# Sorted attention with a feed-forward layer: batch 2's q turned by transposing DMAs, the first output block turned in two parts, the v pieces one place earlier

## The chip, the cores and the metric

The kernel runs on one core of a Trainium2 chip. Its time is the device time of one execution in microseconds. Before the change the median of 5 runs is 237.19 us (236.79 to 237.53). Engines are named as in the profile: PE does the matrix multiplications, PEld is its weight load, DVE, ACT and POOL work on vectors, and SP issues DMAs. POOL issues DMAs too; SP's and POOL's go through separate DMA queues.

## The reference

Four batches of eight heads, 768 rows (S) of 64 columns (D). A small `sort_net` becomes an 8 x 8 mixing matrix P per head through five rounds of exponentials and normalisations. P mixes the eight 96-row blocks of k and of v. Then each 96-row block of q attends to its own mixed block:

```python
k_sorted = np.einsum('bhij,bhjcd->bhicd', P, k_b)     # the same for v
scores = scale * np.matmul(q_b, k_sb.transpose(0, 1, 2, 4, 3))
attn = exp(scores - max) / sum
x = np.matmul(attn, v_sb)      # as 3072 rows x 512 columns
h = x @ w_in                   # 512 -> 2048
g = s * relu(h)**2 + b
out = g @ w_out                # 2048 -> 512, float32
```

## The kernel before

The 3072 rows are cut into eight groups `t` of 384 rows, two per batch. Each group passes through attention (`s_piece` for the scores and their exponentials, `p_piece` for the product with v and its normalisation), a turn of its output X into XT, the first feed-forward product (`ffn1`, L450) and the second (`ffn2`, L494). The order on every engine is the order in which the program is written; no scheduler changes it. A `Queue` (L511) puts attention pieces of later groups into the slots between feed-forward products: `ffn2` calls it after every four matmuls, `ffn1` after every eight.

**How q is turned.** The scores need q with its columns on the partitions (`QT`). Batches 1 and 2 do it on PE: `q_piece` (L261) makes 24 transposes for two head pairs, and DVE or ACT copies the result out of PSUM. Batch 3 does it by DMA: `load_q` (L78) then reads q in six parts of 128 rows with runs of one head's 64 columns, and `q_turn` (L274) issues six transposing DMAs on SP, each waiting for its own part. The other batches' `load_q` is one read with runs of six rows (384 columns).

**How X is turned.** For groups 0 and 1 on PE (`t_piece`, L412), afterwards by one transposing DMA on SP (`x_turn`, L435). For the first two blocks of group 0, `t_piece(0, "v", 0, 2)` at L590 makes eight transposes into one PSUM tile, and DVE copies all of it to XT; `ffn1(0)` starts on that. `warm_up` (L179) puts matmuls on zeros between these steps.

**v of batches 2 and 3.** Six `v_piece2` (the list `V2`) multiply by P, ACT copies the result, and SP writes it to a DRAM tile `dv`. `v_read` (L356) reads it back in the layout the attention needs, in two DMAs per batch. For batches 2 and 3 POOL issues them (L650, L651), after a one-element copy `gate2` (L649) that makes POOL wait for XT[3], the turned output of group 3. After the reads POOL issues `load_q(3)`.

**The stretch the change touches** is the queue of `ffn2(0)` and `ffn2(1)` (L632 to L639), 24 pieces for 24 slots: `q_piece(1, 2)`, batch 1's k pieces, then in slot 6 the loads of k for batches 2 and 3 and of q for batch 2 with `bias_piece`; scores `S2(2, ..)`, `V2`, products `P2(2, ..)`, the DMA turn `T(2)` in slot 18, `q_piece(2, 0)` in slot 21, `T(3)` in slot 23 and `q_piece(2, 2)` in slot 24. Then follow `ffn1(2)`, which needs XT[2], `ffn1(3)`, and `ffn2(2)`, whose first slots hold batch 2's scores `S2(4, 0)` and whose fourth holds `P2(4, 0)`, the first to need `v_read(2)`.

PSUM is used as a ring of three double-bank tiles (`psa`) and a ring of two single-bank tiles (`psb`); the results of `ffn2` lie in `psb` until `flush` (L472) has them scaled by DVE and written out. `flush` starts only when `bias_piece` has made the bias.

Of the kernel before, what the change touches and what calls it, by code (L numbers as in the profile page):

```python
# [10 lines left out]
BF = mybir.dt.bfloat16  # L11
# [7 lines left out]
def kernel(  # L19
# [12 lines left out]
    nc = tc.nc  # L32

    B, H, S, D = q.shape
    NB = sort_net.shape[-1]
    BLK = S // NB
    BH = B * H
    NHP = H // 2
# [4 lines left out]
    TG = HB * BLK  # L43
# [15 lines left out]
    xtp = ctx.enter_context(tc.tile_pool(name="xtp", bufs=2))  # L59
# [6 lines left out]
    psa = ctx.enter_context(tc.tile_pool(name="psa", bufs=3, space=bass.MemoryType.PSUM))  # L66
# [11 lines left out]
    def load_q(b, part=slice(0, 128)):  # L78


        if b == B - 1:
            qr[b] = qrp.tile([128, TQ, H, D], BF, tag="qr", name=f"qr{b}")
            for t in range(TQ):
                nc.gpsimd.dma_start(
                    out=qr[b][:, t],
                    in_=q[b][:, t * 128:(t + 1) * 128, :].rearrange("h p d -> p h d"))
            return
        if b not in qr:
            qr[b] = qrp.tile([128, H, TQ, D], BF, tag="qr", name=f"qr{b}")
        nc.gpsimd.dma_start(  # L90
            out=qr[b][part].rearrange("p h t d -> p h (t d)"),
            in_=q[b].rearrange("h (p t) d -> p h (t d)", t=TQ)[part])

    def load_k(rows, prow, n=1):
        for c0 in range(0, BLK, BLK // n):
            cs = slice(c0, c0 + BLK // n)
            nc.gpsimd.dma_start(out=kb[prow, cs, :], in_=kraw[rows, cs, :])
# [4 lines left out]
    def brows(b):  # L102
        return slice(b * 64, (b + 1) * 64), slice((b % 2) * 64, (b % 2) * 64 + 64)
# [26 lines left out]
    ident = const.tile([128, 128], BF)  # L130
# [21 lines left out]
    for c0 in range(0, d_ff, FCH):  # L152
        w = const.tile([128, NHP, FCH], BF, name=f"wi{c0}")
        nc.gpsimd.dma_start(
            out=w, in_=moe_w_in.rearrange("(hp p) f -> p hp f", p=128)[:, :, c0:c0 + FCH])
# [5 lines left out]
    for f0 in range(0, NF, FW):  # L161
        w = const.tile([128, FW, d_model], BF, name=f"wo{f0}")
        nc.gpsimd.dma_start(
            out=w, in_=moe_w_out.rearrange("(f p) n -> p f n", p=128)[:, f0:f0 + FW, :])
# [14 lines left out]
    def warm_up(n, pool=psb):  # L179
        wp = pool.tile([128, 256], FP, tag="b" if pool is psb else "a", name="wp")  # L180
        for _ in range(n):
            nc.tensor.matmul(out=wp, lhsT=zt[:, 0:128], rhs=zt, start=True, stop=True)  # L182
# [53 lines left out]
    def evac(out, in_, eng):  # L236
        if eng == "v":
            nc.vector.tensor_copy(out=out, in_=in_)  # L238
        else:
            nc.scalar.copy(out=out, in_=in_)  # L240

    QT = {}
# [18 lines left out]
    def q_piece(b, hp0, eng):  # L261

        if hp0 == 0:
            QT[b] = qtp.tile([128, NHP, S], BF, tag="qt", name=f"qt{b}")
        ps = psa.tile([128, 2, 1024], BF, tag="a", name="tq")
        for i in range(2):
            for t in range(TQ):
                for e in range(2):
                    nc.tensor.transpose(  # L269
                        out=ps[e * 64:(e + 1) * 64, i, t * 128:(t + 1) * 128],  # L270
                        in_=qr[b][:, 2 * (hp0 + i) + e, t, :], identity=ident)
        evac(QT[b][:, hp0:hp0 + 2, :].rearrange("q a (p t) -> q a p t", t=TQ),
             ps[:, :, 0:S].rearrange("q a (t p) -> q a p t", t=TQ), eng)

    def q_turn(b):

        QT[b] = qtp.tile([128, NHP, S], BF, tag="qt", name=f"qt{b}")
        for t in range(TQ):
            nc.sync.dma_start(out=QT[b][:, :, t * 128:(t + 1) * 128],
                              in_=qr[b][:, t].rearrange("p h d -> p (h d)"), transpose=True)  # L280
# [75 lines left out]
    def v_read(b, eng):  # L356
        if b > 1:
            new_vs(b)
        src = dv[1] if b == 1 else dv[2][(b - 2) * 64:(b - 1) * 64]
        for cp in range(2):  # L360
            eng.dma_start(out=VS[b][cp * (BLK // 2):(cp + 1) * (BLK // 2), :, 0:D],
                          in_=src.rearrange("g (c two) d -> two c g d", two=2)[cp])

    XT, AT, X = {}, {}, {}
# [16 lines left out]
    def p_piece(t, hp, n0=0, nn=HB):  # L381

        b, half = divmod(t, 2)
        at = AT[t, hp]
        if t not in X:
            X[t] = xp.tile([BLK, HB, d_model], BF, tag="x", name="x")
        x = X[t]
        atf = at.rearrange("p e t -> p (e t)")
        if nn < HB:
            p1 = psb.tile([128, 512], FP, tag="b", name="pv")  # L390
            pv = [p1[:, e * nn * VW:(e + 1) * nn * VW] for e in range(2)]
            pvv = p1[0:BLK, 0:2 * nn * VW].rearrange("p (e n w) -> p e n w", e=2, w=VW)
        else:
            p2 = psa.tile([128, 2, 512], FP, tag="a", name="pv")
            pv = [p2[:, 0], p2[:, 1]]
            pvv = p2[0:BLK, :, 0:nn * VW].rearrange("p e (n w) -> p e n w", w=VW)
        for e in range(2):
            for n in range(n0, n0 + nn):
                c0 = (e * HB + n) * BLK
                m = 128 if c0 + 128 <= 2 * TG else BLK  # L400
                gi = e * 32 + hp * NB + half * HB + n
                nc.tensor.matmul(out=pv[e][0:m, (n - n0) * VW:(n - n0 + 1) * VW],  # L402
                                 lhsT=atf[:, c0:c0 + m],
                                 rhs=VS[b][:, gi, :], start=True, stop=True)
        rec = rtp.tile([BLK, 2, HB], FP, tag="rec", name="rec")
        nc.vector.reciprocal(out=rec[:, :, 0:nn], in_=pvv[:, :, :, D])  # L406
        nc.vector.tensor_tensor(  # L407
            out=x[:, n0:n0 + nn, hp * 128:(hp + 1) * 128].rearrange("p n (e d) -> p e n d", e=2),
            in0=pvv[:, :, :, 0:D],
            in1=rec[:, :, 0:nn].unsqueeze(3).broadcast_to([BLK, 2, nn, D]), op=ALU.mult)  # L410

    def t_piece(t, eng, n0=0, nn=HB):  # L412

        x = X[t]
        if t not in XT:
            XT[t] = xtp.tile([128, NHP, TG], BF, tag="xt", name="xt")
        if nn < HB:
            t1 = psb.tile([128, 1024], BF, tag="b", name="tr")
            tr = [t1[:, hp * nn * BLK:(hp + 1) * nn * BLK] for hp in range(NHP)]
            src = t1[:, 0:NHP * nn * BLK]  # L420
            dst = XT[t][:, :, n0 * BLK:(n0 + nn) * BLK]
            src = src.rearrange("p (a t) -> p a t", a=NHP)
        else:
            t2 = psa.tile([128, 2, 1024], BF, tag="a", name="tr")
            tr = [t2[:, hp // 2, (hp % 2) * TG:(hp % 2 + 1) * TG] for hp in range(NHP)]
            src = t2[:, :, 0:2 * TG]
            dst = XT[t].rearrange("p (a b) t -> p a (b t)", b=2)
        for hp in range(NHP):
            for n in range(n0, n0 + nn):
                nc.tensor.transpose(out=tr[hp][:, (n - n0) * BLK:(n - n0 + 1) * BLK],  # L430
                                    in_=x[:, n, hp * 128:(hp + 1) * 128],
                                    identity=ident[0:BLK, 0:BLK])
        evac(dst, src, eng)

    def x_turn(t):  # L435

        XT[t] = xtp.tile([128, HB * NHP, BLK], BF, tag="xt", name="xt")
        nc.sync.dma_start(out=XT[t], in_=X[t].rearrange("p n m -> p (n m)"), transpose=True)
# [87 lines left out]
    def seq(*fs):  # L526
        def run():
            for f in fs:
                f()
        return run  # L530

    def S2(t, hp):
        return lambda: (s_piece(t, hp), s_piece(t, hp + 1))

    def P2(t, hp):
        return lambda: (p_piece(t, hp), p_piece(t, hp + 1))

    def T(t):
        return lambda: x_turn(t)
# [46 lines left out]
    s_piece(0, 3)  # L586
    for hp in range(NHP):
        p_piece(0, hp, 0, 2)
        warm_up(2, psa)
    t_piece(0, "v", 0, 2)  # L590
    warm_up(2, psa)

    load_v(*brows(2))
# [24 lines left out]
    def csums(f0, f1):  # L618
        for f in range(f0, f1):
            if f == 1:  # L620
                nc.gpsimd.tensor_tensor(out=csum, in0=wo_at(0), in1=wo_at(1), op=ALU.add)
            elif f > 1:
# [8 lines left out]
    V2 = [lambda c0=c0: v_piece2(c0, "s") for c0 in range(0, BLK, 16)]  # L631
    qu = Queue([nothing, lambda: q_piece(1, 2, "v")]  # L632
               + [lambda c0=c0: k_piece(1, c0, 16, 1, "vsv"[c0 // 32])() for c0 in range(0, BLK, 32)]
               + [seq(lambda: load_k(*brows(2)), lambda: load_k(*brows(3)), lambda: load_q(2), bias_piece), S2(2, 0), V2[0], S2(2, 2), V2[1], V2[2], V2[3],
                  P2(2, 0), V2[4], P2(2, 2), V2[5], S2(3, 0),
                  T(2), P2(3, 0), S2(3, 2), lambda: q_piece(2, 0, "v"), P2(3, 2), T(3),
                  lambda: q_piece(2, 2, "v")], 24)
    ffn2(0, qu)
    ffn2(1, qu)  # L639

# [5 lines left out]
    ffn1(2, qu)  # L646
    ffn1(3, qu)
    gate2 = sk.tile([1, 1], BF)
    nc.gpsimd.tensor_copy(out=gate2, in_=XT[3][0:1, 0, 0:1])  # L649
    v_read(2, nc.gpsimd)  # L650
    v_read(3, nc.gpsimd)  # L651
    load_q(3)
# [45 lines left out]
```

## Time and profile before

| | |
|---|---|
| median of 5 runs | 237.19 us |
| the profiled execution's own time | 236.81 us |
| its span | 235.1 us |
| PE busy | 227.7 us (97%) |
| DVE, ACT, POOL busy | 125.3, 111.3, 43.9 us |
| PE, L459 (ffn1) / L502 (ffn2) | 87.9 / 86.7 us |
| PE, L269 (`q_piece`), 96 transposes | 3.4 us |
| mean granted PE clock | 0.978 |

The span is what the profiler saw from the first to the last instruction; 1.7 us of the execution's time lie around it. Times below are microseconds from the span's start. The chain of waits is followed back from the last instruction, at each step to what released it. In a line of the timeline or chain the first number is the start and the second the length; "x8" is a count; a bracket says how long the engine had been idle and what ended that. A DMA has an issue (the time on SP or POOL) and a landing, counted from the start of the issue.

### The profile page before, as it was taken

The page shows a single profiled execution, that of the slowest core. Times are in us where ns is not written, and L with a number is a line of the kernel's source. Part 1 is how long each engine was busy: PE and PEld are TensorE (multiplying, and loading weights), DVE is VectorE, ACT ScalarE, POOL GpSimd, SP SyncE. Part 2 cuts the span into 40 slices and gives each one's busy share as a digit, 9 for nine tenths or more (in the row PEclk, how much of TensorE's full clock was granted, in tenths as well). Part 3 has the DMA queues.
Part 4 walks back from the last instruction along what each step waited for, and adds up shares of the span by engine and source line. Part 5 has one row for each costly group of instructions (what it writes and reads, how often), then busy time and mean ns, then how long its engine had stood idle before and what let it go on. Part 6 is the DMA issues. An engine that isn't in the chain of part 4 may idle for free.

```text
span 235.1 us, 4941 instructions
## 1 busy us (share of the span) xinstructions
PE 227.7 (97%) x2090; PEld 138.0 (59%) x2090; DVE 125.3 (53%) x259; ACT 111.3 (47%) x163; POOL 43.9 (19%) x57
## 2 busy tenths in 40 slices
PE   8979899999999999999999999999999999999994
PEld 5869797765544555555555455655554556554443
DVE  5758665638992658766344654343362544442221
ACT  6158369675148451677766221656322226660000
POOL 7810000299950000494000000000000000000000
PEclk9995699999999999999999999999999999999999
DMA  5799999998699996599992415420024162001112
GB/s 91 112 206 213 225 197 205 230 221 187 93 131 215 270 317 125 121 107 97 122 77 90 112 45 136 90 66 4 0 93 111 53 105 46 0 0 47 59 75 89
DMA packets 38230, 28.11 MB, mean 120 GB/s; under 512 B 26432, under 2 KB 32576, under 8 KB 37696
## 3 DMA queue, kind: packets, MB, share of 16 engines
q0 software_dynamic: 13600, 15.21, 45.2%
q1 hardware_dynamic: 24464, 12.53, 23.1%
q8 instruction: 16, 0.26, 0.5%
q10 hardware_dynamic: 144, 0.07, 0.1%
q14 instruction: 6, 0.05, 0.1%
HBM read 29.63 MB, written 8.65 MB: 163 GB/s over the span
## 4 chain that ended last, share of the span: by engine, by line
PE 83%; DVE 7%; DMA 5%; ACT 2%; issue 1%; POOL 0%; POOLq 0%
PE hps L459 35%; PE ops L502 32%; DMA qr<-in_q_dram 5%; PE pv L402 4%; PE sc L375 3%; DVE gt L464 2%; DVE ks L238 2%; PE tv L320 2%; PE tk L294 2%; PE ops L487 1%; ACT ks L240 1%; PE tv L350 1%; PE tq L269 1%; PE tq L254 1%; PE tv L336 1%
## 5 line engine op out<-in xcount | busy, mean ns | idle before, releaser
L459 PE MATMUL hps<-xt,wi 128*128 128x384 bf16 (+1 forms) x576 | 87.9, 308 | 0.7 <-DVE xt L238 0.4
L502 PE MATMUL ops<-wo,gt 128*128 128x512 bf16 x368 | 86.7, 380 | 0.0
L463 ACT ACTIVATE rt<-hps 128x768 bf16<-128x768 f32 (+1 forms) x72 | 53.2, 740 | 49.0 <-PE hps L459 48.1
L459 PEld LDWEIGHTS <-wi 128*128 128x128 bf16 x576 | 53.4, 98 | 30.6 <-issue 1.9
L464 DVE TENSOR_TENSOR gt<-rt 128x768 bf16<-128x768 bf16 (+1 forms) x72 | 41.2, 574 | 46.2 <-ACT rt L463 45.8
L502 PEld LDWEIGHTS <-gt 128*128 128x128 bf16 x368 | 33.7, 98 | 36.9 <-issue 0.6
L378 ACT ACTIVATE at<-sc 96x768 bf16<-96x768 f32 x32 | 24.4, 803 | 30.5 <-PE sc L375 30.3
L476 DVE SCALAR_TENSOR_TENSOR ot<-ops,s_bc,bias 128x512 f32<-128x512 f32 x23 | 17.2, 749 | 40.4 <-PE ops L502 40.3
L407 DVE TENSOR_TENSOR x<-pv,rec 96x512 bf16<-96x512 f32 (+1 forms) x36 | 22.6, 628 | 1.3
L240 ACT CAST ks<-tk 64x512 bf16<-64x512 f32 (+1 forms) x32 | 16.0, 500 | 6.4 <-PE tk L294 6.1
L238 DVE CAST ks<-tk 64x512 bf16<-64x512 f32 (+1 forms) x32 | 18.1, 565 | 1.3 <-PE tk L294 0.8
L623 POOL TENSOR_TENSOR csum<-csum,wo 128x512 f32<-128x512 f32 x14 | 17.6, 1255 | 1.0
L182 PE MATMUL wp<-zt 128*128 128x256 bf16 x92 | 14.7, 327 | 1.1 <-DVE warm L113 1.1
L402 PEld LDWEIGHTS <-at 96*128 96x128 bf16 (+1 forms) x256 | 12.0, 104 | 3.8
L402 PE MATMUL pv<-vs,at 96*128 96x66 bf16 (+1 forms) x256 | 13.0, 199 | 0.1
L375 PEld LDWEIGHTS <-ks 64*96 64x96 bf16 x256 | 8.5, 128 | 6.5 <-issue 5.7
L182 PEld LDWEIGHTS <-zt 128*128 128x128 bf16 x92 | 10.2, 116 | 3.4 <-DVE warm L113 1.1
L240 ACT CAST vn<-tv 128x512 bf16<-128x512 f32 (+1 forms) x12 | 9.4, 800 | 4.6 <-PE tv L350 3.9
L375 PE MATMUL sc<-qt,ks 64*96 64x96 bf16 x256 | 10.9, 219 | 0.6 <-DVE ks L238 0.5
L406 DVE RECIPROCAL rec<-pv 96x8 f32<-96x8 f32 (+1 forms) x36 | 6.9, 192 | 7.4 <-PE pv L402 7.4
L294 PEld LDWEIGHTS <-kb 64*128 64x128 bf16 x192 | 6.3, 95 | 4.5 <-issue 4.0
L294 PE MATMUL tk<-pd,kb 64*128 64x64 bf16 x192 | 7.8, 191 | 0.0
(70 smaller groups left out, 102.2 us busy)
## 6 DMA issues: line engine op xcount, KB each, us to landing
out_dram<-ot SPq DMA_DIRECT2D x23, 256.0 KB, 2.1
kb<-in_k_dram POOLq DMA_DIRECT2D x4, 768.0 KB, 11.1
vb<-in_v_dram POOLq DMA_DIRECT2D x4, 768.0 KB, 19.7
wi<-in_moe_w_in_dram POOLq DMA_DIRECT2D x2, 1024.0 KB, 20.4
wo<-in_moe_w_out_dram POOLq DMA_DIRECT2D x2, 1024.0 KB, 32.1
qr<-in_q_dram POOLq DMA_DIRECT2D x2, 768.0 KB, 26.6
dv<-vn SPq DMA_DIRECT2D x6, 256.0 KB, 8.0
vs<-dv POOLq DMA_DIRECT2D x4, 384.0 KB, 12.3
```

What stands on the lines that cost most here:

```text
L182: nc.tensor.matmul(out=wp, lhsT=zt[:, 0:128], rhs=zt, start=True, stop=True)
L238: nc.vector.tensor_copy(out=out, in_=in_)
L240: nc.scalar.copy(out=out, in_=in_)
L294: nc.tensor.matmul(out=ps[:, c, :], lhsT=kb[pr, c0 + 2 * c:c0 + 2 * c + 2, :].rearrange("p c d -> p (c d)"), rhs=rhs, start=True, stop=True)
L375: nc.tensor.matmul(out=sc[:, e, n * BLK:(n + 1) * BLK], lhsT=ks[pr, g0 + n, :], rhs=QT[b][pr, hp, q0:q0 + BLK], start=True, stop=True)
L378: nc.scalar.activation(out=at, in_=sc[:, :, 0:TG], func=AF.Exp, scale=scale)
L402: nc.tensor.matmul(out=pv[e][0:m, (n - n0) * VW:(n - n0 + 1) * VW], lhsT=atf[:, c0:c0 + m], rhs=VS[b][:, gi, :], start=True, stop=True)
L407: nc.vector.tensor_tensor(out=x[:, n0:n0 + nn, hp * 128:(hp + 1) * 128].rearrange("p n (e d) -> p e n d", e=2), in0=pvv[:, :, :, 0:D], in1 ...
L459: nc.tensor.matmul(out=hps[:, f, 0:nt], lhsT=wi_at(hp, f0 + f), rhs=xt_at(t, hp, n0, nn), start=(hp == 0), stop=(hp == NHP - 1))
L463: nc.scalar.activation(out=rt[:, :, 0:nt], in_=hps[:, :, 0:nt], func=AF.Relu)
L464: nc.vector.tensor_tensor(out=gt[:, f0:f0 + 2, c0:c0 + nt], in0=rt[:, :, 0:nt], in1=rt[:, :, 0:nt], op=ALU.mult)
L502: nc.tensor.matmul(out=ops, lhsT=gt[:, f, m * 128:(m + 1) * 128], rhs=wo_at(f), start=(f == 0), stop=(f == NF - 1))
```

## The change

Four edits.

- `load_q(2)` takes the form of `load_q(3)` (six DMAs of 128 rows with runs of 64 columns), and `q_turn(2)` in slot 24 replaces the two `q_piece(2, ..)`; slot 21 is left empty.
- `gate2` waits for the last element of QT[2] in place of one of XT[3], so POOL's `v_read(2)`, `v_read(3)` and `load_q(3)` come after `q_turn(2)` has landed.
- The first two blocks of group 0 are turned in two parts: head pairs 0 and 1 by four transposes that ACT copies out, written between `p_piece(0, 3)` and its warm-up, and head pairs 2 and 3 by four that DVE copies out. Each takes a tile of `psa`.
- `V2[0]` and `V2[1]` change places with `S2(2, 0)` and `S2(2, 2)` before them.

```diff
     def load_q(b, part=slice(0, 128)):
-        if b == B - 1:
+        if b > 1:
             qr[b] = qrp.tile([128, TQ, H, D], BF, tag="qr", name=f"qr{b}")
             for t in range(TQ):
                 nc.gpsimd.dma_start(
...
+    def t_part(t, hp0, eng, n0, nn):
+        if t not in XT:
+            XT[t] = xtp.tile([128, NHP, TG], BF, tag="xt", name="xt")
+        tr = psa.tile([128, 2, 1024], BF, tag="a", name="tr")
+        for i in range(2):
+            hp = hp0 + i
+            for n in range(n0, n0 + nn):
+                nc.tensor.transpose(out=tr[:, 0, (i * nn + n - n0) * BLK:(i * nn + n - n0 + 1) * BLK],
+                                    in_=X[t][:, n, hp * 128:(hp + 1) * 128],
+                                    identity=ident[0:BLK, 0:BLK])
+        evac(XT[t][:, hp0:hp0 + 2, n0 * BLK:(n0 + nn) * BLK],
+             tr[:, 0, 0:2 * nn * BLK].rearrange("p (a t) -> p a t", a=2), eng)
...
     for hp in range(NHP):
         p_piece(0, hp, 0, 2)
+        if hp == 3:
+            t_part(0, 0, "s", 0, 2)
         warm_up(2, psa)
-    t_piece(0, "v", 0, 2)
+    t_part(0, 2, "v", 0, 2)
     warm_up(2, psa)
...
-               + [seq(..., lambda: load_q(2), bias_piece), S2(2, 0), V2[0], S2(2, 2), V2[1], V2[2], V2[3],
+               + [seq(..., lambda: load_q(2), bias_piece), V2[0], S2(2, 0), V2[1], S2(2, 2), V2[2], V2[3],
                   P2(2, 0), V2[4], P2(2, 2), V2[5], S2(3, 0),
-                  T(2), P2(3, 0), S2(3, 2), lambda: q_piece(2, 0, "v"), P2(3, 2), T(3),
-                  lambda: q_piece(2, 2, "v")], 24)
+                  T(2), P2(3, 0), S2(3, 2), nothing, P2(3, 2), T(3), lambda: q_turn(2)], 24)
...
-    nc.gpsimd.tensor_copy(out=gate2, in_=XT[3][0:1, 0, 0:1])
+    nc.gpsimd.tensor_copy(out=gate2, in_=QT[2][0:1, NHP - 1, S - 1:S])
     v_read(2, nc.gpsimd)
     v_read(3, nc.gpsimd)
     load_q(3)
```

More of the change, by code (lines that the diff above doesn't have):

```diff
@@ L633 @@
                + [lambda c0=c0: k_piece(1, c0, 16, 1, "vsv"[c0 // 32])() for c0 in range(0, BLK, 32)]
-               + [seq(lambda: load_k(*brows(2)), lambda: load_k(*brows(3)), lambda: load_q(2), bias_piece), S2(2, 0), V2[0], S2(2, 2), V2[1], V2[2], V2[3],
+               + [seq(lambda: load_k(*brows(2)), lambda: load_k(*brows(3)), lambda: load_q(2), bias_piece), V2[0], S2(2, 0), V2[1], S2(2, 2), V2[2], V2[3],
                   P2(2, 0), V2[4], P2(2, 2), V2[5], S2(3, 0),
-                  T(2), P2(3, 0), S2(3, 2), lambda: q_piece(2, 0, "v"), P2(3, 2), T(3),
-                  lambda: q_piece(2, 2, "v")], 24)
+                  T(2), P2(3, 0), S2(3, 2), nothing, P2(3, 2), T(3), lambda: q_turn(2)], 24)
     ffn2(0, qu)
```

## The prediction

> **What bounds the kernel now.** I read the page first, then the chain of waits in order of time, then the timeline around the four edits, then the DMAs' landings and packets.
>
> ```profile
> span 235.1 us, 4941 instructions
> ...
> PE 227.7 (97%) x2090; PEld 138.0 (59%) x2090; DVE 125.3 (53%) x259; ACT 111.3 (47%) x163; POOL 43.9 (19%) x57
> ...
> PE 83%; DVE 7%; DMA 5%; ACT 2%; issue 1%; POOL 0%; POOLq 0%
> ```
>
> PE is 83% of the chain. From 28.67 us it hardly ever stands idle, so a PE instruction taken away there shortens the end by its own length, unless a wait takes its place. The chain shows the places of the edits:
>
> ```profile
> 27.28 0.43 DVE x L407
> 27.71 0.05 issue
> 27.76 0.27 PE tr L430 x2
> 28.03 0.02 issue
> 28.06 0.57 DVE xt L238
> 28.63 0.04 issue
> 28.67 0.82 PE hps L459 x8
> ...
> 88.62 0.79 PE tq L269 x24
> ...
> 92.64 0.79 PE tq L269 x24
> 93.43 1.41 PE hps L459 x8
> ```
>
> The reader sees the first turn (transposes, then one DVE copy, then `ffn1`), and the two `q_piece(2, ..)` at 0.79 us each. The timeline around batch 1's scores and at the two places where a DMA could come late:
>
> ```profile
> 69.88 0.56 PE L375 MATMUL sc<-qt,ks 64*96 64x96 bf16 x15 [0.47 <-DVE ks L238]
> ...
> 70.64 1.55 DVE L476 SCALAR_TENSOR_TENSOR ot<-ops,s_bc,bias 128x512 f32<-128x512 f32 x2
> ...
> 71.67 0.59 PE L502 MATMUL ops<-wo,gt 128*128 128x512 bf16 x2
> ...
> 96.85 0.18 POOL L649 COPY gate<-xt 1x1 bf16<-1x1 bf16 x1 [28.75 <-DMA xt<-x]
> ...
> 121.34 0.80 PEld L402 LDWEIGHTS <-at 96*128 96x128 bf16 x16
> ```
>
> The scores waited 0.47 us for DVE; POOL's gate opened at 96.85; 121.34 is `P2(4, 0)`, the first user of `v_read(2)`. Last, the DMAs: the two turns of X (issue time, then landing) and the packets of 79 to 82 us and of 117 to 122.5 us.
>
> ```profile
> L438 SPq DMA_TRANSPOSE xt<-x x1: 2926/2926/2926, 84.4 to 84.4; - x1
> DMA to landing us min/median/max: 7.0/7.0/7.0
> ...
> L438 SPq DMA_TRANSPOSE xt<-x x1: 1294/1294/1294, 92.9 to 92.9; - x1
> DMA to landing us min/median/max: 3.9/3.9/3.9
> ...
> DMA packets 667, 0.86 MB, mean 287 GB/s; under 512 B 38, under 2 KB 373, under 8 KB 667
> ...
> DMA packets 3963, 0.52 MB, mean 94 GB/s; under 512 B 3962, under 2 KB 3962, under 8 KB 3962
> ```
>
> XT[2] lands at 84.4 + 7.0 = 91.4, only 2.0 us ahead of `ffn1(2)` at 93.36, in a stretch in which the DMA engines are full. This is the tightest place.
>
> **The change part by part.**
>
> *The q pieces go.* 48 transposes, 2 x 0.79 = 1.58 us of PE on the chain. Their two DVE copies (1.76 us each) lie off it. PE loses nothing for `q_turn(2)`. Taken: -1.58. A gain smaller than this means a new wait, costed below.
>
> *The first turn.* Now DVE copies 384 elements, not 768. Its rows are 550 ns for 768 and 944 for 1536, so 0.51 ns an element, and the copy takes 0.36: 0.20 less. The ACT half is off the path: ACT idles 3.69 us before 29.53, and a 384-wide ACT row is 0.49. Its transposes stand ahead of the last warm-ups, so it is done near 27.9. By the built order, the first matmul of `ffn1` waits for ACT only and the third for DVE, so two of the eight matmuls of 0.82 us (0.20) move ahead of the DVE copy. Together -0.40. Bounds: 0, if the added `psa` tiles make a transpose wait for a warm-up, and -0.6, the whole copy. No wait on data further on takes it back: the second half of w_in landed at 8.0 + 22.7 = 30.7, needed at 32.1.
>
> *v ahead of the scores.* `V2[0]` (0.43 us on the chain) fills PE's wait for ks, which is 0.47 (0.68 from the first score matmul to the second); the scores then come a slot later, when ks is ready. What is late next: the third row block of `ffn2(0)` reuses the `psb` tile that DVE's first `flush` frees. That runs after ks and bias, from 70.64 for half of 1.55, so until 71.41, and no edit moves DVE here. The block began at 71.67 and can now begin near 71.46: -0.20. Bounds 0 and -0.68. The V2 copies on ACT and the dv writes on SP come 1.4 us sooner; the exponentials of the two scores come a slot later, with five slots to spare before `P2(2, 0)`.
>
> Sum of the gains: 1.58 + 0.40 + 0.20 = 2.18 us.
>
> *The strided q load.* POOL now issues six DMAs of 0.9 us (5.4) in place of one of 0.91. Behind them on POOL stands only the gate, which waits until 97 anyway. The k loads are ahead, so they do not move. But the load is heavier on the DMA engines. The same load for batch 3 is alone at 117 to 122.5: 5.5 us x 16 engines / 3963 packets = 22 ns a packet. Its 6144 runs of 128 bytes make 384 packets an engine, 8.5 us of all engines; the old form took 9.2 us beside other traffic (batch 3's k landed 66.7 + 12.5 = 79.2, q at 67.2 + 21.2 = 88.4), of which about 4 were its own. So some 4 us of work join a full stretch. [...]
>
> Who pays? SP's queue (dv writes, outputs, then the turn of X[2]) shares the engines with this load. In 79 to 82 us, 335 packets have 512 B to 2 KB (q's old 768 B runs) and 294 more: about one for one, whatever their size. With 128-byte packets in q's place each turn is shorter (62 ns becomes 22), so SP's queue should drain faster and q itself should pay. Against that, a turn of X is small packets too and then gets half. The need: `ffn1(2)` starts 2.18 sooner, at 91.18. With the k and q loads 0.40 earlier, as POOL's work follows X[1], an unchanged queue lands XT[2] at 91.0. Bounds of the stall: 0, and 3.8 if all 4 us fall on the turn of X (95.0). I take 0.3, near the lower end, because of the packet counts.
>
> *q_turn(2) and the gate.* `T(3)` is issued near 91.3, then an output, then six turns. Batch 3's six: first issue 144.4, last 151.6, landing 2.5 later, 9.7 in all. From 93.2 that is 102.9. The load's last part, should it land at 95 to 98, is ready before its own turn's issue near 100.4. Nothing on SP is due behind them before `ffn2(2)`'s first output near 120. XT[3] goes first, due near 102. The gate opens at 102.9 instead of 96.85, 6.1 later; behind it on POOL stand `v_read(2)`, `v_read(3)` and `load_q(3)`. `v_read(2)`'s second half landed at 99.0 + 10.8 = 109.8, now 115.9; `P2(4, 0)` needs it at 121.34 - 2.2 = 119.2: 3.3 us to spare. `v_read(3)` (117.5, now 124) is needed near 168, q of batch 3 (122.4, now 129) at 142. Cost 0; bounds 0 and 3, if the gate comes 6 us later than this. [...] The row shows a turn among full queues at 7.0 instead of 3.9, so in time the two do meet.
>
> **Sum.** 236.81 - 2.18 + 0.3 = 234.9 for the profiled execution. The median of the five runs lies 0.38 above it, so 235.3 as a median.
>
> **The rivals.**
>
> 1. *The turn of X[2] comes late, and the kernel gets slower.* For it: full DMA engines from 66 to 91 us, 4 us more work, the slack used up by the gain itself. Against it: the packet counts. It decides from a landing of XT[2] at 93.4 (all gain gone) and gives slower beyond 93.8; at its worst, 95.0, the time is 237.19 - 2.18 + 3.8 = 238.8. Chance 0.22, of which 0.13 slower, 0.06 no change, 0.03 a smaller gain.
> 2. *The gate opens late* and `P2(4, 0)` waits. Needs QT[2] after 106.2; each further us costs one. At 109 the time is 237.8. Against it: batch 3's six turns took 9.7 us. Chance 0.10 (0.06 slower, 0.02, 0.02).
> 3. *The front gains do not arrive* (`psa` waits, DVE's chain to 71.4), and 0.3 is lost at XT[2]: 237.19 - 1.58 + 0.3 = 235.9, or, with a wait of 1 us somewhere, 236.9. Chance 0.08 (0.06 faster, 0.02 none).
>
> **How the numbers follow.** The forecast has 0.60, all faster. Faster by over 0.2% (0.47 us, about what a measurement of this kernel can tell): 0.60 + 0.03 + 0.02 + 0.06 = 0.71; within: 0.06 + 0.02 + 0.02 = 0.10; slower: 0.13 + 0.06 = 0.19. The low end takes the upper bounds of all gains (1.58 + 0.6 + 0.68 = 2.86) and no stall: 234.3, taken as 234.4. The high end, 237.5, leaves out most of the slower cases, some 0.17.
>
> **What would show it.** Right: no L269 transposes after 62 us, `ffn1(0)` under way by 28.3, the third row block near 71.0 on the new clock of events, `ffn1(2)` starting near 91.3 with at most 0.5 us waited for xt, the gate near 103, no wait ahead of `P2(4, 0)`. Wrong: PE idle at the start of `ffn1(2)` on the DMA xt for over 1 us; PE idle near 119 on the DMA vs; the first weight load of `ffn1(0)` not earlier than 28.6. What I trust least is how the DMA engines divide between the strided load and the turn of X[2].

## The result: slower, with the gain used up by a wait

The changed kernel takes 238.88 us as the median of its runs (236.65 at the lowest), the kernel before 237.18. The ratio of the undisturbed runs is 1.0041, 95% interval [1.0026, 1.0057]: slower by 0.4%. Some executions are disturbed and take longer throughout: medians here are of all runs, ratios of the undisturbed ones. Forecast were 235.3 and faster, with a range up to 237.5. The undisturbed times fall into groups that go with the mean granted PE clock: five runs at 0.978 take 236.65 to 236.95 us, three at 0.971 take 237.07 to 237.63, sixteen at 0.964 take 238.53 to 239.35. A step of 0.007 is some 3.3 us at half clock in a span of 235. The profiled execution took 239.07 us at 0.964; its span is 237.4.

The page of the changed kernel, its head and its shares of the chain:

```profile
span 237.4 us, 4859 instructions
...
PE 228.0 (96%) x2042; PEld 138.1 (58%) x2042; DVE 121.8 (51%) x257; ACT 111.8 (47%) x164; POOL 48.2 (20%) x62
...
PEclk9985599999999999799999999999999999999999
...
PE 80%; DMA 9%; DVE 7%; ACT 2%; issue 1%; POOL 0%; POOLq 0%
...
L473 PE MATMUL hps<-xt,wi 128*128 128x384 bf16 (+1 forms) x576 | 89.9, 313 | 2.4 <-DMA xt<-x 2.1
```

PE executes 48 matmuls fewer (2042 for 2090) and is still busy as long: 228.0 us for 227.7. The turn of X, a DMA, has joined the chain (DMA 9% for 5%), PE waits 2.1 us for it, and one slice in the middle shows a granted clock of 0.7. The chain of the changed kernel in order of time:

```profile
27.78 0.33 PE tr L443 x4
28.10 0.43 PE wp L182 x2
28.53 1.28 PE hps L473 x8
29.81 0.15 PE pv L402 x4
29.96 0.66 PE hps L473 x8
...
70.96 0.76 DVE ot L490
71.72 0.04 issue
71.77 1.02 PE ops L516 x4
...
84.01 0.48 PE ops L516 x2
84.49 9.41 DMA xt<-x
93.90 0.05 issue
93.95 2.17 PE hps L473 x8
96.12 0.54 PE tk L294 x8
96.66 3.37 PE hps L473 x16
100.03 0.34 PE tk L294 x8
...
234.04 0.03 issue
```

The chain of the kernel before, at the last places compared:

```profile
95.17 2.71 PE hps L459 x16
97.88 0.34 PE tk L294 x8
...
231.88 0.03 issue
```

XT[2] is issued at 84.49 (before: 84.40) but lands 9.41 us later instead of 7.0, at 93.90. Set against the kernel before, the third row block of `ffn2(0)` stands at +0.10 us (71.77 for 71.67); PE is ready for `ffn1(2)` at 93.95 - 2.12 = 91.83, so at -1.60 (before: 93.43); it starts at +0.52; and two k pieces later it stands at +2.15 (100.03 for 97.88). From there nothing changes any more: +2.16 at the end (234.04 for 231.88). So the wait took 2.12 us of a lead of 1.60, and the 1.63 us after it came from something else. The same stretch by windows of 2 us; the columns are the stretch, its length, the busy time and count of PE, PEld, DVE, ACT and POOL, the granted clock, the DMA share and GB/s:

```profile
92.00:94.00 2.00, 0.05 (x1) 0.05 (x2) 0.62 (x1) 0.00 (x0) 0.00 (x0) 1.00 1.20 212
94.00:96.00 2.00, 2.00 (x8) 0.81 (x8) 0.00 (x0) 0.00 (x0) 0.00 (x0) 0.64 1.38 90
96.00:98.00 2.00, 2.00 (x14) 1.19 (x14) 0.98 (x3) 0.81 (x1) 0.00 (x0) 0.50 1.21 324
98.00:100.00 2.00, 2.00 (x14) 1.02 (x13) 1.56 (x4) 0.81 (x1) 0.00 (x0) 1.00 0.43 87
```

PE stands still from 91.83 to 93.95. Soon after it starts again, its clock is halved: 0.64 in one window and 0.50 in the next make 3.4 us at half clock, from about 94.6 to 98.0. The first eight matmuls of `ffn1(2)` take 2.17 us instead of 1.41.

### The profile page after: what moved, and what is told of

Same layout as the page of the kernel before. It is cut to its first block, busy times and chain, and to the rows that moved or that the text cites. A ratio compares the mean times of both kernels' runs of the same rounds, so it can differ in the third digit from the quotient of the medians.

```text
span 237.4 us, 4859 instructions
## 1 busy us (share of the span) xinstructions
PE 228.0 (96%) x2042; PEld 138.1 (58%) x2042; DVE 121.8 (51%) x257; ACT 111.8 (47%) x164; POOL 48.2 (20%) x62
## 4 chain that ended last, share of the span: by engine, by line
PE 80%; DMA 9%; DVE 7%; ACT 2%; issue 1%; POOL 0%; POOLq 0%
PE hps L473 35%; PE ops L516 29%; DMA qr<-in_q_dram 5%; DMA xt<-x 4%; PE pv L402 3%; PE sc L375 3%; DVE gt L478 2%; DVE ks L238 2%; PE tv L320 2%; PE tk L294 2%; PE ops L501 1%; ACT ks L240 1%; PE tv L350 1%; PE wp L182 1%; PE tq L254 1%
## 5 line engine op out<-in xcount | busy, mean ns | idle before, releaser
L473 PE MATMUL hps<-xt,wi 128*128 128x384 bf16 (+1 forms) x576 | 89.9, 313 | 2.4 <-DMA xt<-x 2.1
L473 PEld LDWEIGHTS <-wi 128*128 128x128 bf16 x576 | 54.3, 99 | 33.4 <-DMA xt<-x 2.6
L84 POOL DMA_DIRECT2D qr<-in_q_dram x12 | 10.6, 903 | 3.4 <-DMA vs<-dv 3.3
```

Of the source, the lines that this page charges most:

```text
L473: nc.tensor.matmul(out=hps[:, f, 0:nt], lhsT=wi_at(hp, f0 + f), rhs=xt_at(t, hp, n0, nn), start=(hp == 0), stop=(hp == NHP - 1))
```

## The experiments

Theory D: the strided load of q shares the full DMA engines with SP's queue, the turn of X[2] lands late, PE waits, and the wait is followed by a stretch of half clock. Rivals: F, the loss comes from the first turn; G, the turn is late because of SP's own queue; H, the small packets beside the turn hurt and not the amount of work. Each time stands against the median of the kernel before on the same chip; ratios have 95% intervals.

### One edit at a time

```diff
-        if b == B - 1:        # only_q: this, q_turn(2) and the gate on QT[2], nothing else
+        if b > 1:
```

> The kernel before with only the q edit: strided load of batch 2's q, its six transposing DMAs, and POOL's reads held back until they landed. Theory D (the strided load shares the DMA engines with the turn of X[2], PE waits at the start of ffn1(2), and a stretch of half granted clock follows that wait): XT[2] lands near 93.9 as in the changed kernel, PE waits about 2 us there, the clock is 0.5 for about 3.4 us after it; about 238.7 to 239.3 us in runs with that clock loss and 237.3 to 237.7 without. Rival F (the loss comes from the first turn in two parts, whose added steps keep the clock low longer, and the q edit by itself gains its 1.58 us of PE): 235.6 us.

237.68 us (237.41 to 239.60) against 237.38, ratio 1.0030 [1.0008, 1.0051]. Theory D: nine of twelve runs lie between 237.41 and 237.82, three from 239.04 up. The profiled run is of the first group (237.53); its chain, and its clock after the wait:

```profile
84.42 9.53 DMA xt<-x
93.94 0.05 issue
93.99 1.47 PE hps L473 x8
```

```profile
94.00:96.00 2.00, 2.00 (x18) 1.18 (x19) 0.00 (x0) 0.50 (x1) 0.00 (x0) 1.00 0.84 92
```

The same wait (2.23 us), this time at full clock. So the wait comes with the q edit alone, which loses already without the clock; and the half clock follows the wait in some executions only. Rival F's 235.6 is out.

```diff
-    t_piece(0, "v", 0, 2)      # only_turn: with the four transposes behind p_piece(0, 3), too
+    t_part(0, 2, "v", 0, 2)
```

> The kernel before with only the first turn in two parts. Theory D: ffn1(0) starts some 0.3 to 0.4 us sooner where the clock returns at the same point as before; 236.8 to 237.2 us. Rival F: the clock comes back one stretch later (near 29.6 instead of 27.3), the second group of ffn1(0) is 0.3 us later than before, 237.5 to 238 us in all runs.

237.02 us against 237.38, ratio 0.9991 [0.9975, 1.0008]: not told from no change. Its profiled run starts the second group of `ffn1(0)` at 29.45, 0.18 sooner than the kernel before, although in it the clock was low until 28.7 and not until 27.3. The point where the first low stretch ends differs from run to run, in kernels with the old first turn too (27.3 before, about 28.9 in only_v), so the changed kernel's 29.96 isn't a loss that the edit was shown to cause.

```diff
-... S2(2, 0), V2[0], S2(2, 2), V2[1], V2[2] ...      # only_v
+... V2[0], S2(2, 0), V2[1], S2(2, 2), V2[2] ...
```

> The kernel before with only the v pieces ahead of batch 1's scores. Both theories: the wait for ks goes, and the third row block of ffn2(0) waits for DVE's first flush instead, so 0.1 to 0.2 us gained at most: 237.0 to 237.2 us. If the flush were not the limit: 236.6.

237.42 us against 237.38, ratio 1.0006 [0.9987, 1.0025]: nothing. The timeline of that run shows a wait that can take the 0.2 us back:

```profile
87.49 1.04 PE L502 MATMUL ops<-wo,gt 128*128 128x512 bf16 x4
89.19 0.86 PE L269 MATMUL tq<-ident,qr 128*64 128x128 bf16 x24 [0.67 <-DMA qr<-in_q_dram]
```

The old q load landed at 67.3 + 21.8 = 89.1 (88.4 before), and `q_piece(2, 0)`, free to start at 88.5, waits for it. The changed kernel has no such piece.

### The clock

```diff
+    warm_up(16)      # filler: 16 matmuls on zeros where PE waits for XT[2]
     ffn1(2, qu)
```

> The changed kernel with 16 matmuls on zeros (about 1.7 us) written in front of ffn1(2), where PE waits for XT[2]. They do no work; they only keep PE busy during the wait. Theory D with the wait as the cause of the low clock: the start of ffn1(2) stays at 93.9, no half-clock stretch follows, and the slow cluster of the changed kernel's times (238.5 to 239.4) disappears: 236.7 to 237.4 us. If the low clock has another cause, or if its length does not depend on the wait: as the changed kernel, 238.9.

237.44 us against 237.38, ratio 1.0007 [0.9991, 1.0022]. Work that is of no use brought the changed kernel's ratio from 1.0041 to 1.0007, at the same start of `ffn1(2)`:

```profile
91.89 1.91 PE L182 MATMUL wp<-zt 128*128 128x256 bf16 x16
94.07 1.47 PE L473 MATMUL hps<-xt,wi 128*128 128x384 bf16 x8 [0.26 <-DMA xt<-x]
```

The clock stays at 1.00 there, and but for one run at 238.70 the group from 238.5 to 239.4 is gone. So the half clock behind this wait comes from PE standing still, though not in every execution: only_q's profiled run waits 2.23 us and stays at 1.00. Five of the profiled runs below have slow matmuls behind a wait of PE, too, whatever it waited for. Behind XT[2] (2.11 us in no_hold, 2.2 in q_first) the first eight matmuls of `ffn1(2)` take 2.65 and 2.26 us, for 1.47 here. Behind POOL's sums (4.96 us in early, 2.3 in early_nohold) the two matmuls that make the bias take 2.07 and 2.08 us, for 1.03 in the changed kernel. The fifth is k3_late_nohold. In the changed kernel 2.12 us were enough in the profiled run, and in two undisturbed runs out of three if the sixteen at 0.964 are those that paid. Why one execution pays and the next doesn't is not shown by any run here.

### Moving the strided load

```diff
     load_v(*brows(2))
+    load_q(2)      # early: here, not in slot 6 (early_nohold: the gate on XT[3] as well)
```

> The changed kernel with batch 2's strided q load issued much sooner on POOL, right behind the load of batch 2's v (near 34 us, when the tile's last reader is done), instead of behind the k loads at 67.5; nothing else moves. Theory D (the strided load delays the turn of X[2]): XT[2] lands by 90, ffn1(2) starts near 91.8 without a wait and without a half-clock stretch, and the gain of the q edit arrives: 235.0 to 235.7 us. Rival G (the turn of X[2] is late because of SP's own queue, the dv writes and outputs, or for another reason that stays): XT[2] still near 93.5 to 94, 236.8 to 238.9 us. A risk of the move itself: batch 3's v, whose load now stands behind this one, lands after 69 and V2[0] waits for it.

240.33 us against 237.35, ratio 1.0123 [1.0084, 1.0162], so slower still, and for a reason that none of the theories named. XT[2] is no longer waited for; it lands 4.1 us after its issue, and `ffn1(2)` follows `ffn2(1)` without a gap. But POOL's issues wait for older loads one after the other, the last until 50.82, and the column sums of w_out, which the bias needs, start and end late:

```profile
43.43 0.87 POOL L84 DMA_DIRECT2D qr<-in_q_dram  x1 [2.98 <-DMA qr<-in_q_dram]
50.82 0.87 POOL L84 DMA_DIRECT2D qr<-in_q_dram  x1 [6.51 <-DMA wo<-in_moe_w_out_dram]
...
71.91 2.07 PE L560 MATMUL bps<-csum,onesf 128*128 128x512 f32 x2 [4.96 <-POOL csum L640]
```

Theory D holds at XT[2], rival G falls (SP's queue had the same transfers), and the move costs a wait of 5 us for POOL, behind which the two matmuls for the bias take 2.07 us for 1.03.

```diff
-    nc.gpsimd.tensor_copy(out=gate2, in_=QT[2][0:1, NHP - 1, S - 1:S])
+    nc.gpsimd.tensor_copy(out=gate2, in_=XT[3][0:1, 0, 0:1])      # no_hold
```

> The changed kernel with POOL's gate on XT[3] again, so the reads of v are not held back until QT[2] landed. Theory D: nothing changes at the start of ffn1(2), the wait of about 2 us and the low clock stay: 237 to 239 us, as the changed kernel. The gate opens near 97; the six transposing DMAs of q share the engines with the reads and land later than 103.8, but well before the scores at 120. If the hold had a price of its own: 1 us or more faster. If the transposing DMAs suffer from the reads: PE waits at 120 for QT[2].

238.60 us against 237.35, ratio 1.0027 [0.9999, 1.0056], not told from no change nor from the changed kernel: of the nine undisturbed runs five lie between 236.88 and 237.31 and four between 238.56 and 239.79. XT[2] lands after 9.4 us, as there. But the last two transposing DMAs of q, beside the reads of v, now take 23.4 and 23.9 us to land, instead of 2.4 to 2.5. The scores at 119.5 need only the first three parts, which landed within 3.5 us, so PE did not wait.

> Both moves together: the strided load early, and the gate on XT[3]. Theory D: as with the early load alone within 0.2 us, 235.0 to 235.7 us, since the reads have over 3 us to spare either way. If the reads disturb the transposing DMAs so that PE waits at 118: slower than the early load alone by that wait.

239.47 us against 237.35, ratio 1.0069 [1.0043, 1.0094]. In its profiled run PE waits 2.3 us for POOL's sums (5.0 in the run above) and not at all for XT[2].

```diff
-... seq(lambda: load_k(*brows(2)), lambda: load_k(*brows(3)), lambda: load_q(2), bias_piece) ...
+... seq(lambda: load_q(2), lambda: load_k(*brows(2)), lambda: load_k(*brows(3)), bias_piece) ...      # q_first
```

> The changed kernel with the strided q load issued ahead of the two k loads in the same slot; the same work in the same stretch, in another order: the last part of it, beside the turn of X[2], is then k in long runs. Theory D (the amount of work in the stretch): XT[2] still lands near 93 to 94, 237 to 239 us. Rival H (small packets beside the turn): XT[2] lands near 91, no wait, 235.2 to 235.8 us. If long runs crowd the turn out more than short ones: later than 94.

237.26 us against 237.49, ratio 1.0013 [0.9987, 1.0039]. In its profiled run (239.27 us) PE waits 2.2 us for XT[2], which lands at 94.1, although q has gone by (POOL's queue has 2 packets in all from 85 to 88 us):

```profile
L452 SPq DMA_TRANSPOSE xt<-x x1: 2319/2319/2319, 86.7 to 86.7; - x1
...
DMA to landing us min/median/max: 7.4/7.4/7.4
```

Here SP issued the turn only at 86.7; from 79 to 82 us its queue had moved 0.12 MB beside k's long runs (0.54 MB in 60 packets), for 0.76 MB in the changed kernel. So XT[2] can be late without small packets beside its turn, but here it is late in another way: its issue came late. That doesn't settle rival H for the changed kernel. Only four of twelve runs lie above 238.5, and two at 236.3 suggest that some executions of this order wait less; no profile of them was taken.

### Taking work out of the full stretch

```diff
-... seq(lambda: load_k(*brows(2)), lambda: load_k(*brows(3)), lambda: load_q(2), bias_piece) ...
+... seq(lambda: load_k(*brows(2)), lambda: load_q(2), bias_piece) ...
...
+    load_k(*brows(3))      # k3_late: behind the gate on QT[2]
     v_read(2, nc.gpsimd)
```

> The changed kernel with batch 3's k load taken out of the full stretch: issued by POOL behind the gate on QT[2], ahead of the reads of v, and not at 67; nothing runs on POOL in its place, so the bias is not delayed. It was about 3.6 us of the DMA engines' work (75.6 to 79.2), about what the strided q load added. Theory D: XT[2] lands near 90.5 again, PE waits under 0.5 us at ffn1(2), no half-clock stretch there: 235.2 to 236.0 us, if the reads of v, now some 4 us later (near 120), still come before P2(4, 0) near 119 to 121; each us they are late is paid. Rival H (it is not the amount of work in the stretch but the small packets beside the turn that slow it): XT[2] lands still over 92.5, the wait stays over 1 us.

235.06 us (234.65 to 236.44) against 237.49, ratio 0.9906 [0.9886, 0.9925]: faster than both kernels, by 0.9%. Nothing of the change was undone; batch 3's k, which is first used near 117 us, just isn't loaded in the crowded stretch. The chain and the turn of X[2]:

```profile
89.42 0.54 PE pv L402 x16
89.96 1.73 PE ops L516 x8
91.68 1.30 PE hps L473 x8
```

```profile
L452 SPq DMA_TRANSPOSE xt<-x x1: 2132/2132/2132, 84.3 to 84.3; - x1
...
DMA to landing us min/median/max: 4.6/4.6/4.6
```

XT[2] lands at 88.9, and `ffn1(2)` starts at 91.68 without a wait. `P2(4, 0)` at 119.86 is not held up by the later reads. This run doesn't tell theory D from rival H either: with less work in the stretch, q's packets had gone by, too, before the turn was issued.

> The kernel before with only batch 3's k load moved behind its gate on XT[3]. In it nothing waits for XT[2], so theory D gives no gain: 237.0 to 237.5 us; XT[2] lands some 3 us sooner, near 88. If this alone were faster by 1 us, a gain of the run with the q edit would not be due to XT[2].

237.09 us against 237.49, ratio 0.9985 [0.9976, 0.9994]. The late k in the kernel before is worth about 0.4 us; the gain of the run above isn't its own.

> As the run with batch 3's k loaded late, and POOL's gate on XT[3] as in the kernel before, so the k load and the reads of v start near 96 and the transposing DMAs of q share the engines with them. Theory D: no wait at ffn1(2) as there; the reads are in time for P2(4, 0), but the transposing DMAs get slow beside the reads (without the hold the slowest took 23.9 us to land), so PE may wait for QT[2] at 118: 235.2 to 236 us if not, about 1 us per us of that wait if so.

238.40 us against 237.49, ratio 1.0037 [1.0010, 1.0065]. Without the hold, a transposing DMA of q beside the k load and the reads takes 21.8 us, and now PE needs it:

```profile
118.24 0.47 PE L375 MATMUL sc<-qt,ks 64*96 64x96 bf16 x12 [2.58 <-DMA qt<-qr]
```

The hold, which looked superfluous, is worth about 3 us once the rest is mended (238.40 for 235.06). In its profiled run the matmuls behind that wait are slow: four of `ffn2` take 1.40 us from 118.71 and the next eight 2.57, for 1.73 the next time (from 124.17).

> The kernel before with the q edit and batch 3's k loaded late, without the other two edits. It sizes the terms of the sum where XT[2] is not waited for. Theory D: PE's 1.58 us come through whole against the control with only the late k (237.09): 235.5 us; the run with all edits and late k (235.06) then owes some 0.4 us to the first turn and the v pieces. If the q edit alone gives 235.1, those two edits are worth nothing; if it gives 236.5 or more, the q edit has another price and the first turn is worth more than it seemed.

235.39 us against 237.31, ratio 0.9915 [0.9901, 0.9929]. Against the control (237.09) the q edit gives 1.70 us, for the 1.58 of the forecast (the two ran on different chips; their ratios give 1.66). The first turn and the v pieces together would add 0.33 (to 235.06), for 0.60, but the intervals of these two runs overlap, so that part stays open. In the profiled run some of q's load still ran beside the turn of X[2]. The DMA view of 84 to 88 us, first here, then in k3_late; q0 is POOL's queue, q1 SP's, and the columns are packets, MB and the packets' time as a share of 16 engines:

```profile
q1 hardware_dynamic: 926, 0.90, 104.8%
q0 software_dynamic: 1618, 0.20, 79.7%
...
q1 hardware_dynamic: 1572, 0.87, 102.8%
q0 software_dynamic: 23, 0.00, 1.1%
```

The turn landed 6.4 us after its issue here and 4.6 in k3_late; in the changed kernel, with 3802 packets of q in these 4 us, it took 9.4. So in these three runs XT[2] is the later, the more of the strided load is still moving beside it. Whether their number or their smallness does it (D or H) stays open.

## Why the prediction was wrong

- **The step that failed is "Who pays?".** It took 0.3 us for the wait at XT[2], near the lower end of its 0 to 3.8, "because of the packet counts". The wait is 2.12 us. The inference, from 335 packets beside 294 in one stretch of 3 us, was that the queues go on packet for packet, so that the 128-byte packets of q would cost SP's queue little. For a while the counts are like that. The DMA view of the changed kernel, 78 to 80 us:

```profile
q1 hardware_dynamic: 320, 0.58, 86.9%
q0 software_dynamic: 317, 0.04, 30.5%
```

Up to 84 us SP's queue even drained faster, as was said: from 75 to 84 us it moved 1.81 MB, for 1.43 before. But then an output, a dv write and the turn of X[2] stand in it; the changed kernel from 84 to 88 us, and the kernel before:

```profile
q0 software_dynamic: 3802, 0.48, 187.8%
q1 hardware_dynamic: 179, 0.31, 23.7%
...
q1 hardware_dynamic: 628, 1.06, 75.5%
q0 software_dynamic: 324, 0.24, 37.9%
```

Twenty-one of q's packets go to one of SP's, and SP's queue moves 0.31 MB where it had moved 1.06. So the count of one for one, which the kernel before showed from 79 to 82 us (335 of POOL's queue, 332 of SP's), doesn't hold through the stretch; the load went ahead and the turn behind it paid. What makes the engines change over stays open.
- **The 4 us of added work, the upper bound of that step, were mis-sized as well.** The 22 ns a packet were taken over 117 to 122.5 us, but the load keeps its pace only until about 119.5: from there to 122.5 the engines move 49 GB/s. The DMA view of the kernel before, 117 to 119.5 us:

```profile
DMA packets 2907, 0.37 MB, mean 147 GB/s; under 512 B 2907, under 2 KB 2907, under 8 KB 2907
```

2.5 us x 16 engines / 2907 packets = 13.8 ns. By it the load is an estimated 5.3 us and not 8.5, and against the 4 us taken for the old form (itself an estimate) it adds some 1.3. That is less than the 2.4 us by which the turn was later, so by this estimate the amount alone doesn't explain the delay.
- **What PE pays for standing still was not in the sum at all.** The wait costs its own length (2.12 us), and in the profiled run 1.63 us more at half clock; its mean clock of 0.964 is that of sixteen of the 24 undisturbed runs. Without the clock rival 1, with the measured landing of 93.9, gives 237.19 - 2.18 + (93.9 - 91.18) = 237.7 us, as the first group of only_q has it (237.41 to 237.82); the median of 238.88 has the clock on top. The eight runs of the changed kernel below 237.7 (from 236.65) lie mostly lower than this sum; none of them was profiled, so how long PE waited in them isn't known.
- **Rival 1 was the right one**, with its place (the start of `ffn1(2)`) and the point from which it decides (slower beyond a landing of 93.8). The error was its chance of 0.22. The working had found that the slack of 2.0 us was used up by the gain itself and that work joined engines that were full; nothing but the packet count spoke against it. But the landing of 93.9 alone makes it only just slower, by 0.5 us; the rest of the loss is the clock, which this rival didn't have.
- **The gains were right in sum.** Where the wait is taken away, 2.43 us come through against the kernel before (235.06 for 237.49) and 2.03 against the control, for a predicted 2.18. The q pieces: 1.70 for 1.58. The other two edits are not shown to give their 0.60: each by itself could not be told from no change. In the changed kernel the third row block waits 0.41 us on DVE's `flush`, as was said of the v pieces, and DVE's half of the first copy takes the 0.36 us that were worked out. In the profiled run the clock, low until 29.7, hid the gain of that copy.
- **The q turns and the gate were right.** The gate opened at 103.78 (102.9 predicted), q's last part landed at 94.5 (95 to 98), no reader of v waited. That a turn and full queues meet in time was right as well: without the hold the slowest turn of q beside these reads takes 23.9 us to land (no_hold), and 21.8 with batch 3's k load beside it as well (k3_late_nohold), where in the changed kernel they take 2.4 to 3.5.

## What to carry to other kernels

Saving PE work moved the moment at which the next input is needed by 1.60 us here (91.83 for 93.43), while the transfer at the end of the full queue was issued when it had been before (84.49 for 84.40): subtract the saving from the slack first, and charge the work that the change adds to a full stretch to the transfer that ends last in it. A gap of 2.12 us on PE cost another 1.63 us in granted clock in the changed kernel's profiled run, and one of 2.23 us in only_q's cost none, so price such a gap both ways, or fill it. Then look for a load in that stretch that is not needed for long: moving one turned a loss of 0.4% into a gain of 0.9%.

## What was not expected of the hardware

- 2.12 us without matmuls were followed by 3.4 us at half the granted clock in the changed kernel's profiled run, whose mean clock of 0.964 is that of sixteen of the 24 undisturbed runs; with 16 matmuls on zeros in the gap (filler) the clock stayed at 1.00.
- The last two transposing DMAs of q, which land in 2.4 to 2.5 us in the changed kernel, took 23.4 and 23.9 us beside the reads of v (no_hold); the slowest of those reads took 22.1 us to land instead of 15.8.
- Of six DMAs issued on POOL in a row (early), the last three each stood still until an older load had landed (3.33, 2.98 and 6.51 us), 17 us from the first to the last (33.6 to 50.8), and held up the vector work behind them.
